# VectorE writes K's transposed blocks with the two heads apart, and the scores read 64-byte runs

## The chip, the cores and the metric

The kernel runs on one core of one Trainium2 chip. The metric is the device time of one execution in microseconds (us). The core's engines are named as the profile names them: PE (TensorE, matmuls), PEld (its weight loads), DVE (VectorE), ACT (ScalarE), POOL (GpSimd) and SP (SyncE, which issues nearly all transfers). SBUF is the on-chip memory of 128 partitions, psum the accumulators that matmuls write, and HBM the memory off the chip.

## What is computed

Two attention blocks with cached K and V are computed from inputs of their own, and their outputs are joined along the last axis. Block A has 32 query heads that share 4 heads of K and V; block B has 32 heads of each. In both there are 16 batches of 32 tokens, 1024 model columns, 1024 cached positions and heads of 128 columns, all in bf16.

```python
def _B_ref(x, k_cache, v_cache, wq, wo):      # x 16x32x1024, k_cache and v_cache 16x32x1024x128
    q = (x @ wq).reshape(B, Sq, H, Dh).transpose(0, 2, 1, 3)
    scores = einsum("bhqd,bhkd->bhqk", q, k_cache) * Dh ** -0.5
    p = softmax(scores, axis=-1)
    o = einsum("bhqk,bhkd->bhqd", p, v_cache)
    return o.transpose(0, 2, 1, 3).reshape(B, Sq, H * Dh) @ wo
# _A_ref: the same with 4 heads of k_cache and v_cache, each repeated 8 times
return concatenate([A, B], axis=-1)
```

## The kernel before

Each of the two blocks is cut into 128 steps. A step of A (a quad) takes four query heads of one batch, a step of B two heads of two neighbouring batches; in both these are 128 rows of scores. Two steps of B with the other two of four heads and the same batches form a pair, so B has 64 pairs. The loop in `build` goes through B's pairs and A's quads side by side, and adds the projections of the queries (L735, L754), the output projections (L823) and the loads of weights between them. What is added this way is only a list of operations with their dependences. `list_schedule` then orders the whole list once, before the program is written: it prices each operation by the table `DUR`, each transfer by `PACKET`, and gives every engine a fixed order. `emit_all` writes the engines' programs in that order, with semaphore waits where one engine needs another's result. The change alters no name, dependence or price, so the order stays as it is.

K of B is needed with the head's 128 columns on partitions. A pair needs K of four heads in two batches, which comes in two loads of 1 MB, one for each batch (`st_dmaKB`, L912), each into two neighbouring slots of KB_sb; late in the kernel some go into wq_sb. One load brings four heads `(i e)` of a batch:

```python
src = pb["k"][...].rearrange("(i e) (r s) d -> (e r) i (s d)", e=2, s=32)
```

A partition is made up of e, r and i, with i the innermost: within each 32 partitions there are sixteen r, and for each both heads i = 0 and 1 side by side. Along a partition lie 32 positions s of 128 columns d. `st_ktrB` (L982) then lets VectorE transpose each slot in place as 4-byte words, in blocks of 32x32 (L983). A word is two neighbouring columns d, w = 0 and 1. After it a partition stands for a pair of columns, and the 32 words of a block stand for 16 positions r of head i = 0 and 1 in turn.

`st_scoresB` (L1018) multiplies the queries with it. For each of four passes `fp` (which half of the blocks, and which of the two columns in a word) it issues 16 matmuls on 32x32 tiles of TensorE, each with 512 streamed columns (32 positions s times 16 positions r): four row groups, one for each e and half of the 32 r, times four x, which are the two batches (x // 2) and i = x % 2. Each x takes the words of its own i alone, so its 2-byte elements stand 8 bytes apart. The four passes add up in the same psum banks (L1035).

The scores then go to `st_max` (the maximum on VectorE, L1046), `st_exp` (exp and its sum on ScalarE, L1059), `st_ptB` (TensorE transposes of the probabilities, L1105), copies out of psum on either engine (L651) and the product with V (`st_pvB`, L1124). A's quads take the same way by L976, L1002, L1046, L1059, L1071 and L1091. The queries of B are turned by a smaller transpose on VectorE (L765) and by matmuls with an identity (L778). x is turned at the start by L671, and B's outputs by L1198. SyncE issues the loads in its own order and waits for slots to come free: L912 for K of B, L962 for V of B, L891 and L898 for K and V of A.

Of the kernel before, what the change touches and what calls it, by code (L numbers as in the profile page):

```python
# [11 lines left out]
F32 = mybir.dt.float32  # L12
# [540 lines left out]
def build(nc, pa, pb, out):  # L553
# [32 lines left out]
    pr = Prog()  # L586
    stack = contextlib.ExitStack()
    with stack:
# [35 lines left out]
        def bank(v):  # L624
            return psum[:, v.idx, :]
# [308 lines left out]
        def home_k(x):  # L934
            if x < XK:
                return ("KB", x % NKB)
            return ("wq", (x - XK) % (NKB + 4)) if (x - XK) % (NKB + 4) < 4 else ("KB", kb_of(x))

        def tile_k2(x):
            kind, sl = home_k(x)  # L940
            assert x % 2 == 0 and sl % 2 == 0 and home_k(x + 1) == (kind, sl + 1)
            return (wq_sb[:, 2 * sl:2 * sl + 4, :] if kind == "wq" else KB_sb[:, sl:sl + 2, :]).rearrange("p j c -> p (j c)")

        def tile_k(x):
            kind, sl = home_k(x)
            return wq_sb[:, 2 * sl:2 * sl + 2, :].rearrange("p j c -> p (j c)") if kind == "wq" else KB_sb[:, sl, :]
# [33 lines left out]
                 wtag={("KTA", sl): q.kid})  # L980

        def st_ktrB(x):  # L982
            pr.add("dve", lambda e: e.transpose(tile_k(x).bitcast(F32), tile_k(x).bitcast(F32)),  # L983
                   writes=[home_k(x)], name="KBt_tr", rtag={home_k(x): x}, wtag={home_k(x): ("T", x)})

        def both(vS):
# [2 lines left out]
        def score_buf(q):  # L989
            q.vS = [Virt("bank", "S"), Virt("bank", "S")]  # L990
            q.vst, q.vbo = Virt("stat"), Virt("bank")
# [24 lines left out]
        def st_scoresB(qs):  # L1016
            n = qs[0].pn
            vP, vPT = (("xT", 0, 0), (("xT", 0, 1), ("xT", 0, 2))) if n >= XT_FREE and n % 2 else (Virt("P2"), (Virt("PT2"), Virt("PT2")))  # L1018
            for q in qs:
                score_buf(q)  # L1020
                q.vP, q.vPT, q.vO = vP, vPT, Virt("O2")
            q0 = qs[0]
            gp = (q0.m * NG + q0.G) % 2

            def e_s(e, fp):
                last = None
                o0 = (fp // 2) * 64 + fp % 2
                for x in range(4):
                    for q in qs:
                        for g2 in range(2):  # L1030
                            r0 = 32 * (2 * q.e + g2)
                            lhsT = QR[r0:r0 + 32, gp, 2 * q.bp + x // 2, x % 2, o0:o0 + 63:2]
                            k2 = tile_k2(4 * q.pn + x // 2 * 2)[r0:r0 + 32, :].rearrange("p (s x) -> p s x", s=32)
                            rhs = k2[:, :, o0 + 2 * (x % 2):(fp // 2) * 64 + 64:4]
                            last = e.matmul(bank(q.vS[g2])[32 * x:32 * x + 32, :].rearrange("p (s j) -> p s j", s=32), lhsT, rhs,  # L1035
                                            start=(fp == 0), stop=(fp == 3), tile_position=(r0, 32 * x))
                return last
            qr = [("QR", gp, 2 * q0.bp + t_) for t_ in range(2)]
            kt = [(home_k(4 * q0.pn + x), ("T", 4 * q0.pn + x)) for x in range(4)]
            for fp_ in range(4):  # L1040
                pr.add("pe", lambda e, fp_=fp_: e_s(e, fp_), reads=qr + [r_ for r_, _ in kt], writes=[r_ for q in qs for r_ in q.vS],
                       name="scoresB", tag="B%d" % q0.t, rtag=dict([(r_, (q0.m, q0.G)) for r_ in qr] + kt))
# [174 lines left out]
        def pairB(n):  # L1217
            qs = [quadsB[2 * n], quadsB[2 * n + 1]]
            for x in range(4):
                st_ktrB(4 * n + x)  # L1220
            if n == 0:
                for x in range(4, NKB):
                    st_dmaKB(x)
            st_scoresB(qs)
            while k_next[0] < min(2 * NIT, 4 * n + 4 + NKB + (4 if n >= LATE else 0)):
                st_dmaKB(k_next[0])
                k_next[0] += 1
            if 4 * n == V_LAST - 8:
                for x in (0, 2, 1, 3):
                    st_dmaVB(V_LAST + x)  # L1230
            for q in qs:
                st_max(q)
                st_exp(q)
            st_ptB(qs)
            if 4 * n == V_LAST:
                st_last(qs)
                return
            st_pvB(qs)
            while v_next[0] < min(V_LAST, 4 * n + 4 + NVB + (4 if n >= LATE else 0)):
                st_dmaVB(v_next[0])  # L1240
                v_next[0] += 1
            for q in qs:
                st_recip(q)
                st_norm(q)
                st_otr(q)
# [122 lines left out]
        if SCHED:  # L1368
            pr = pr.list_schedule()
# [41 lines left out]
```

## Time and profile before

| | before |
|---|---|
| median of 3 runs | 895.69 us (893.65 to 896.92) |
| the profiled execution's own time | 897.08 us |
| its span | 895.3 us |
| mean granted TensorE clock | 0.996 |
| PE, DVE, ACT busy | 819.3, 741.0, 617.9 us |
| moved by DMA | 341.66 MB, mean 382 GB/s |

The span runs from the first to the last instruction; the profiled execution's own time is 1.8 us more. Busy times of engines overlap. In the groups of instructions, a row names line, engine, operation, output<-inputs and shapes, then the count, the busy time in all, the mean duration of one in ns, and the idle time of the engine just before them with what ended it. A busy time counts overlapping matmuls once, so it is less than count times duration. A few matmul records can be missing.

### The profile page before, as it was taken

The page shows a single profiled execution, that of the slowest core. Times are in us where ns is not written, and L with a number is a line of the kernel's source. Part 1 is how long each engine was busy: PE and PEld are TensorE (multiplying, and loading weights), DVE is VectorE, ACT ScalarE, POOL GpSimd, SP SyncE. Part 2 cuts the span into 40 slices and gives each one's busy share as a digit, 9 for nine tenths or more (in the row PEclk, how much of TensorE's full clock was granted, in tenths as well). Part 3 has the DMA queues.
Part 4 walks back from the last instruction along what each step waited for, and adds up shares of the span by engine and source line. Part 5 has one row for each costly group of instructions (what it writes and reads, how often), then busy time and mean ns, then how long its engine had stood idle before and what let it go on. Part 6 is the DMA issues. An engine that isn't in the chain of part 4 may idle for free.

```text
span 895.3 us, 29488 instructions
## 1 busy us (share of the span) xinstructions
PE 819.3 (92%) x12925; PEld 530.3 (59%) x13056; DVE 741.0 (83%) x1039; ACT 617.9 (69%) x1342; POOL 6.1 (1%) x20
## 2 busy tenths in 40 slices
PE   7988999999999999899999999999999998989786
PEld 4445565666665666556666665656656655666554
DVE  0588888788888798887998887998898888899875
ACT  4477687777766775676766777576767667787744
POOL 0000000000000000000000000000000000000000
PEclk9999999999999999999999999999999999999999
DMA  9999999999999999899999999899999999999990
GB/s 338 414 381 392 418 400 383 403 362 386 393 416 387 372 395 382 352 364 410 363 412 371 413 372 391 344 417 394 363 419 404 379 398 413 395 418 417 421 378 37
DMA packets 93775, 341.66 MB, mean 382 GB/s; under 512 B 10000, under 2 KB 10256, under 8 KB 77264
## 3 DMA queue, kind: packets, MB, share of 16 engines
q1 hardware_dynamic: 93088, 337.94, 95.5%
q8 instruction: 103, 1.69, 0.7%
q0 software_dynamic: 560, 1.84, 0.5%
q14 instruction: 24, 0.20, 0.1%
HBM read 337.64 MB, written 2.10 MB: 379 GB/s over the span
## 4 chain that ended last, share of the span: by engine, by line
PE 64%; ACT 15%; DVE 14%; DMA 4%; issue 2%; SPq 1%; DVEq 0%; ACTq 0%
PE psum L1035 14%; PE psum L823 10%; ACT P_sb L1059 9%; DVE stat L1046 9%; PE psum L1124 9%; PE psum L1105 5%; PE psum L1071 5%; PE psum L735 5%; PE psum L1091 4%; PE psum L754 4%; PE psum L1002 4%; DVE KB_sb L983 3%; DMA VB_sb<-in_B_v_cache_dram 2%; PE psum L976 2%; ACT O_sb L1182 1%
## 5 line engine op out<-in xcount | busy, mean ns | idle before, releaser
L1046 DVE TENSOR_REDUCE stat<-psum 128x1 f32<-128x1024 f32 x256 | 305.2, 1215 | 80.1 <-PE psum L1035 51.9
L1059 ACT ACTIVATE P_sb<-psum,stat 128x1024 bf16<-128x1024 f32 x246 | 275.5, 1120 | 104.5 <-DVE stat L1046 101.3
L983 DVE STREAM_TRANSPOSE KB_sb<-KB_sb 128x1024 f32<-128x1024 f32 x240 | 285.6, 1220 | 14.3 <-DMA KB_sb<-in_B_k_cache_dram 14.2
L651 ACT COPY PT_sb<-psum 128x512 f32<-128x512 f32 x217 | 125.4, 601 | 40.2 <-PE psum L1071 21.2
L1035 PE MATMUL psum<-KB_sb,QR 32*32 32x512 bf16 x3840 | 125.9, 630 | 5.9 <-ACT P_sb L1059 3.3
L1124 PE MATMUL psum<-VB_sb,PT_sb 64*64 64x256 bf16 x3584 | 116.6, 271 | 7.5 <-ACT P_sb L1059 3.1
L1124 PEld LDWEIGHTS psum<-VB_sb,PT_sb 64*64 64x64 bf16 x3584 | 96.5, 107 | 29.1 <-issue 26.5
L1182 ACT ACTIVATE O_sb<-psum,stat 128x128 bf16<-128x128 f32 (+1 forms) x197 | 78.8, 418 | 42.7 <-PE psum L1091 27.6
L1071 PE MATMUL psum<-id,P_sb 128*128 128x128 f32 x512 | 89.1, 298 | 7.1 <-ACT P_sb L1059 3.6
L1071 PEld LDWEIGHTS psum<-id,P_sb 128*128 128x128 f32 x512 | 73.6, 208 | 26.6 <-ACT P_sb L1059 13.2
L1091 PE MATMUL psum<-VA_sb,PT_sb 128*128 128x128 bf16 x1024 | 77.9, 219 | 5.4 <-ACT P_sb L1059 2.0
L1105 PE MATMUL psum<-id,P_sb 128*128 128x128 f32 x472 | 76.8, 288 | 6.1 <-ACT P_sb L1059 5.0
L1091 PEld LDWEIGHTS psum<-VA_sb,PT_sb 128*128 128x128 bf16 x1024 | 62.9, 98 | 30.8 <-issue 11.1
L1035 PEld LDWEIGHTS psum<-KB_sb,QR 32*32 32x32 bf16 x3840 | 50.1, 89 | 52.0 <-issue 21.0
L1002 PE MATMUL psum<-KTA_sb,QT_sb 128*128 128x512 bf16 x202 | 68.8, 380 | 6.8 <-ACT P_sb L1059 2.3
L1105 PEld LDWEIGHTS psum<-id,P_sb 128*128 128x128 f32 x472 | 64.6, 194 | 16.9 <-ACT P_sb L1059 7.6
L754 PE MATMUL psum<-wq_sb,xT_sb 128*128 128x512 bf16 x239 | 68.6, 388 | 4.5 <-DMA wq_sb<-in_B_wq_dram 2.2
L823 PE MATMUL psum<-woB_sb,OTB_sb 128*128 128x512 bf16 x234 | 62.4, 379 | 4.6 <-issue 1.6
L823 PE MATMUL psum<-woA_sb,OTA_sb 128*128 128x512 bf16 x241 | 61.2, 388 | 3.0 <-issue 1.4
L735 PE MATMUL psum<-xT_sb,wq_sb 128*128 128x512 bf16 x170 | 48.2, 379 | 2.5 <-issue 1.8
L1059 ACT ACTIVATION_READ_ACCUMULATOR P_sb<-psum,stat 128x1 f32 x246 | 49.7, 202 | 0.0
L835 DVE TENSOR_TENSOR acc<-acc,psum 128x512 f32<-128x512 f32 x64 | 41.1, 675 | 6.2 <-PE psum L823 5.9
(74 smaller groups left out, 737.0 us busy)
## 6 DMA issues: line engine op xcount, KB each, us to landing
KB_sb<-in_B_k_cache_dram SPq DMA_DIRECT2D x120, 1024.0 KB, 8.6
VB_sb<-in_B_v_cache_dram SPq DMA_DIRECT2D x234, 512.0 KB, 8.1
KA_sb<-in_A_k_cache_dram SPq DMA_DIRECT2D x64, 256.0 KB, 7.3
VA_sb<-in_A_v_cache_dram SPq DMA_DIRECT2D x64, 256.0 KB, 7.4
wq_sb<-in_B_wq_dram SPq DMA_DIRECT2D x16, 512.0 KB, 8.0
woB_sb<-in_B_wo_dram SPq DMA_DIRECT2D x32, 256.0 KB, 8.9
woA_sb<-in_A_wo_dram SPq DMA_DIRECT2D x32, 256.0 KB, 7.7
wq_sb<-in_B_k_cache_dram SPq DMA_DIRECT2D x8, 1024.0 KB, 12.0
```

The lines of the kernel that those rows point to most:

```text
L651: return e.copy(dst, src) if hasattr(e, "activation") else e.tensor_copy(dst, src)
L754: last = e.matmul(bank(v)[:, 0:CW], xT_sb[:, 1, j, G * P:(G + 1) * P], wq_sb[:, j, mh * CW:(mh + 1) * CW], start=(j == 0), stop=(j == DJ - 1))
L823: last = e.matmul(bank(v)[:, 0:OUTW], OT[:, gp, hh, :], wo_[:, hh, oh * OUTW:(oh + 1) * OUTW], start=(hh == 0), stop=(hh == nh - 1))
L983: pr.add("dve", lambda e: e.transpose(tile_k(x).bitcast(F32), tile_k(x).bitcast(F32)), writes=[home_k(x)], name="KBt_tr", rtag={home_k(x): ...
L1002: pr.add("pe", lambda e, u=u: e.matmul(bank(vS[u]), qt[:, q.b, q.hh0:q.hh0 + 4, :].rearrange("p a q -> p (a q)"), KTA_sb[:, sl, u * 512:(u ...
L1035: last = e.matmul(bank(q.vS[g2])[32 * x:32 * x + 32, :].rearrange("p (s j) -> p s j", s=32), lhsT, rhs, start=(fp == 0), stop=(fp == 3), t ...
L1046: pr.add("dve", lambda e: e.tensor_reduce(stat[:, vst.idx, 0:1], both(vS), AXIS.XY, ALU.max, negate=True), writes=vS + [vst], name="max")
L1059: return e.activation(dst, src, ACTF.Exp, bias=stat[:, vst.idx, 0:1], scale=1.0, accum_out=stat[:, vst.idx, 1:2])
L1071: last = e.transpose(bank(vb)[:, m * P:(m + 1) * P], p32[:, m:Sk // 2:NPK], id32[:])
L1091: last = e.matmul(bank(vb)[:, 0:Dh], ptc_of(vPT, c, 0, P), VA_sb[:, kvs, c, :], start=(c == 0), stop=(c == NCH - 1))
L1105: last = e.transpose(bank(vb)[:, m * P:(m + 1) * P], p32[:, 4 * h + m:Sk:8], id32[:])
L1124: last = e.matmul(bank(q.vbo)[n0:n0 + 64, 0:2 * Dh].rearrange("p (i d) -> p i d", i=2), pt2_chunk(vPT, c, e0, n0), v2[e0:e0 + 64, :, c, :] ...
```

## The change

VectorE's transpose of a slot of K reads as before but writes through another pattern: within each block of 32 words, word 2b + i goes to place 16i + b. So a block holds the 16 positions of head i = 0 in its first 64 bytes and those of head i = 1 in the other 64. The scores of x read the half with i = x % 2: for each s and each half f, 16 elements of 2 bytes that stand 4 bytes apart, within 64 bytes. Number and sizes of instructions, transfers and buffers stay the same.

```diff
         def st_ktrB(x):
-            pr.add("dve", lambda e: e.transpose(tile_k(x).bitcast(F32), tile_k(x).bitcast(F32)),
+            def emit(e):
+                t32 = tile_k(x).bitcast(F32)
+                return e.transpose(t32.rearrange("p (k i b) -> p k b i", i=2, b=16), t32.rearrange("p (k b i) -> p k b i", i=2, b=16))
+            pr.add("dve", emit,
                    writes=[home_k(x)], name="KBt_tr", rtag={home_k(x): x}, wtag={home_k(x): ("T", x)})
...
                             lhsT = QR[r0:r0 + 32, gp, 2 * q.bp + x // 2, x % 2, o0:o0 + 63:2]
-                            k2 = tile_k2(4 * q.pn + x // 2 * 2)[r0:r0 + 32, :].rearrange("p (s x) -> p s x", s=32)
-                            rhs = k2[:, :, o0 + 2 * (x % 2):(fp // 2) * 64 + 64:4]
+                            k2 = tile_k2(4 * q.pn + x // 2 * 2)[r0:r0 + 32, :].rearrange("p (s f i b w) -> p s f i b w", s=32, f=2, i=2, b=16)
+                            rhs = k2[:, :, fp // 2, x % 2, :, fp % 2]
```

## The prediction

> **What bounds the kernel now.** I read the page first, then the busy time in three stretches, then the waits of VectorE and of SyncE's queue.
>
> ```profile
> span 895.3 us, 29488 instructions
> ## 1 busy us (share of the span) xinstructions
> PE 819.3 (92%) x12925; PEld 530.3 (59%) x13056; DVE 741.0 (83%) x1039; ACT 617.9 (69%) x1342; POOL 6.1 (1%) x20
> ...
> GB/s 338 414 381 392 418 400 383 403 362 386 393 416 387 372 395 382 352 364 410 363 412 371 413 372 391 344 417 394 363 419 404 379 398 413 395 418 417 421 378 37
> ...
> q1 hardware_dynamic: 93088, 337.94, 95.5%
> ...
> ## 4 chain that ended last, share of the span: by engine, by line
> PE 64%; ACT 15%; DVE 14%; DMA 4%; issue 2%; SPq 1%; DVEq 0%; ACTq 0%
> PE psum L1035 14%; PE psum L823 10%; ACT P_sb L1059 9%; DVE stat L1046 9%; PE psum L1124 9%; PE psum L1105 5%; PE psum L1071 5%; PE psum L735 5%; PE psum L1091 4%; PE psum L754 4%; PE psum L1002 4%; DVE KB_sb L983 3%; DMA VB_sb<-in_B_v_cache_dram 2%; PE psum L976 2%; ACT O_sb L1182 1%
> ```
>
> Three things stand near their limit together: TensorE is busy for 92% of the span, VectorE for 83%, and the main DMA queue for 95.5% of the sixteen engines' time. The chain that ended last runs mostly over TensorE, and its largest single line is the scores of B, L1035, with 14% of 895.3 us, or 125 us. DMA is 4% of that chain.
>
> ```profile
> 0.00:40.00 40.00, 32.79 (x217) 16.69 (x236) 10.20 (x11) 16.28 (x24) 2.15 (x13) 1.00 0.97 374
> 40.00:840.00 800.00, 744.15 (x11928) 487.16 (x12017) 692.58 (x973) 574.25 (x1260) 2.31 (x4) 1.00 0.99 391
> 840.00:895.30 55.30, 42.38 (x800) 26.45 (x804) 38.22 (x57) 27.38 (x60) 1.63 (x3) 0.94 0.61 248
> ```
>
> The columns are the length, the busy time of PE, PEld, DVE, ACT and POOL, the granted clock, the DMA share and GB/s. The middle stretch of 800 us is the steady state. VectorE works 692.6 us of it and stands idle for 107.4 us. That idle time is all that VectorE can take up before it sets the pace itself. TensorE is idle there for 55.9 us, and the DMA share is 0.99. The clock is full, so every duration below can be compared with every other.
>
> ```profile
> DVE stat L1046 <- PE psum L1035: 51.9, 50, 3.0
> DVE stat L1046 <- PE psum L1002: 17.3, 30, 2.4
> DVE KB_sb L983 <- DMA KB_sb<-in_B_k_cache_dram: 14.2, 11, 5.3
> ```
>
> Half of VectorE's spare time is spent waiting for the scores of B: 51.9 us in 50 waits, or 1.04 us each. VectorE hardly ever waits for K itself (14.2 us).
>
> ```profile
> SPq L962 <- PE psum L1124: 128.3, 43, 9.8
> SPq L891 <- PE psum L976: 76.5, 29, 6.6
> ```
>
> SyncE's queue waits for TensorE to release buffers (128.3 us for V of B alone, 76.5 us for K of A). So TensorE decides when most loads start, although the DMA engines are almost never empty.
>
> **The scores: what the change gives.** The rows of one line, grouped by shape, and one run of it in the timeline:
>
> ```profile
> L1035 PE MATMUL psum<-KB_sb,QR 32*32 32x512 bf16 x3840 | 125.9, 630 | 5.9 <-ACT P_sb L1059 3.3 <-ACT OTB_sb L651 0.7 <-ACT OTA_sb L651 0.5
> L1002 PE MATMUL psum<-KTA_sb,QT_sb 128*128 128x512 bf16 x202 | 68.8, 380 | 6.8 <-ACT P_sb L1059 2.3 <-issue 1.0 <-ACT PT_sb L651 0.9
> L778 PE MATMUL psum<-QBt,ident 32*32 32x256 bf16 x512 | 20.0, 279 | 3.0 <-ACT PT_sb L651 0.7
> L1198 PE MATMUL psum<-rowsel,O_sb 128*128 128x128 bf16 x252 | 27.3, 220 | 1.2 <-ACT O_sb L1182 0.8
> ```
>
> ```profile
> 398.14 2.11 PE L1035 MATMUL psum<-KB_sb,QR 32*32 32x512 bf16 x64 [0.48 <-ACT P_sb L1059]
> ```
>
> ```profile
> 40.00:840.00 800.00, 125.59 (x3840) 49.95 (x3808) 1.00 0.99 391
> 840.00:895.30 55.30, 8.28 (x256) 3.36 (x256) 0.94 0.61 248
> ```
>
> One score step of a pair is 64 matmuls on 32x32 tiles, four (the four passes `fp`) behind one another on each of 16 tiles. One takes 630 ns with 512 columns. On contiguous operands 512 columns take 380 ns (L1002) and 128 columns 220 ns (L1198), so a column costs 160/384 = 0.417 ns, and 256 columns should take 273 ns. L778 uses the same 32x32 tiles with contiguous moving columns and takes 279 ns for 256. So the small tile costs nothing, and the 250 ns that L1035 takes above 380 ns come from how it reads K: one 2-byte element every 8 bytes. The run of 64 in 2.11 us says the same: (2.11 - 0.63)/3 = 0.49 us from pass to pass, where 512 columns at 0.417 ns are 0.213 us.
>
> After the change the step is 4 bytes, sixteen elements in 64 bytes. No matmul row in the trace moves its streamed operand at this step. The weights of L1035 itself are read at a 4-byte step, which gives no price for a stream. The bounds are therefore no gain (630 ns stay) and the full 250 ns; I take the full one, since the data per element is as dense as can be without repacking the two halves of a word, and half the step should at least halve a cost that comes with the step. A run then loses 4 x 0.25 = 1.0 us, and all 64 runs lose 64 us of TensorE's 819. The middle stretch holds 3840/64 = 60 recorded runs, 60 us. None of this appears in the time unless VectorE keeps up.
>
> The Trainium skill, "SBUF — State Buffer", section "Door 1: The DMA port swizzle", says that two hits on one 16-byte line are enough for full bandwidth. An 8-byte step has two hits per line, so by that rule the scores would be at full rate already and this part would give nothing; the 630 ns against 380 ns speak against it.
>
> **The transposes: what the change costs.** Every one of the 256 transposes of K (240 in KB_sb, 16 in wq_sb) keeps its source order and its count. Its destination changes: two successive elements of a block, which lay 4 bytes apart, now go to places 64 bytes apart, then 60 bytes back, and so on through all 1024.
>
> ```profile
> L983 DVE STREAM_TRANSPOSE KB_sb<-KB_sb 128x1024 f32<-128x1024 f32 x240 | 285.6, 1220 | 14.3 <-DMA KB_sb<-in_B_k_cache_dram 14.2
> L765 DVE STREAM_TRANSPOSE QBt<-Qtok 128x256 f32<-128x256 f32 x32 | 13.6, 426 | 15.1 <-ACT Qtok L649 13.3 <-PE psum L778 1.8
> ```
>
> ```profile
> 0.00:40.00 40.00, 4.74 (x4) 1.00 0.97 374
> 40.00:840.00 800.00, 282.49 (x238) 1.00 0.99 391
> 840.00:895.30 55.30, 16.89 (x15) 0.94 0.61 248
> ```
>
> From 256 to 1024 elements the time grows from 426 to 1220 ns, or 1.034 ns per element, with 162 ns fixed. The streamed part is 1059 ns. No VectorE row in this trace writes with such hops, so I price it from both sides. The cheap side is another engine's stream that hops 64 bytes and more, in PSUM:
>
> ```profile
> L1059 ACT ACTIVATE P_sb<-psum,stat 128x1024 bf16<-128x1024 f32 x246 | 275.5, 1120 | 104.5 <-DVE stat L1046 101.3
> L651 ACT COPY PT_sb<-psum 128x512 f32<-128x512 f32 x217 | 125.4, 601 | 40.2 <-PE psum L1071 21.2 <-PE psum L1105 17.0
> L651 ACT CAST OTB_sb<-psum 128x128 bf16<-128x128 f32 x110 | 25.9, 280 | 7.3 <-PE psum L1198 6.7
> ```
>
> ScalarE's exp reads its 1024 scores across the grain. Its copies and casts, which read in longer runs, grow by (601 - 280)/384 = 0.84 ns per element; on to 1024 elements that gives 1029 ns, and exp takes 1120 ns. A hop costs at most 0.09 ns per element there. Carried to VectorE this is 0.09 us per transpose, and the lower bound is nothing at all. I exclude a gain: the count is the same and the destination only less orderly. The dear side is TensorE reading SBUF:
>
> ```profile
> L671 PEld LDWEIGHTS psum<-ident,acc 128*128 128x128 bf16 x64 | 5.2, 152 | 4.3 <-DMA acc<-in_B_x_dram 3.7 <-issue 0.3
> L976 PEld LDWEIGHTS psum<-ident,KA_sb 128*128 128x128 bf16 x512 | 31.6, 98 | 9.6 <-issue 5.5 <-DMA KA_sb<-in_A_k_cache_dram 1.3
> ```
>
> L671 loads 128 columns at a 16-byte step in 152 ns, where L976 loads contiguous ones in 98 ns. That is 0.42 ns more per element, or 1.55 times. L1035 above pays (0.49 - 0.213)/512 = 0.54 ns per element, or 2.3 times. Carried over as nanoseconds, these are 0.43 and 0.55 us per transpose; as factors on 1059 ns they are 0.58 and 1.38 us. I take 0.58 us, the factor of L671: it is the row in which, as in the new write, every element lies in another 16 bytes than the one before, in the same memory. A transpose then takes 1.80 us. The ends are 0 and 1.38 us.
>
> The Trainium skill, "Vector Engine (DVE) Microarchitecture Reference", section "5.2 Measured stream behaviour on trn2", holds that a VectorE port keeps its rate only in runs of two or more adjacent words. Its figures for a hopping destination are 1.71 to 2.50 ns per element against 1.054, so by estimate 0.66 to 1.45 us more per transpose, and in the sum below 993 to 1190 us. It reports too that one source alternating between two regions ran at full rate, and no row here shows a hopping write of VectorE.
>
> **The sum, against the profiled execution.** In the middle stretch VectorE then works 692.6 + 238 x 0.58 = 831 us, more than the 800 us that the stretch has, so it becomes the bound. Its order is fixed, so the maxima (L1046), the reciprocals and the accumulations of both halves stand queued behind the longer transposes; behind the maxima wait ScalarE's exps, then TensorE, and SyncE's loads behind TensorE. No wait is added and no instruction or transfer is moved. Of its idle 107.4 us the 51.9 us of waiting for scores go, because runs are 1 us shorter and a late VectorE finds them done. Of the other 55 us I keep 40: some are waits for TensorE and DMA that shrink when VectorE is late, some are round trips that stay. The middle takes 831 + 40 = 871 us, 71 more. Outside it, four transposes stand ahead of the first scores, and about eight on the path at the end: 12 x 0.58 = 7 us, less two score runs, 2 us; 5 us more. The span is 895.3 + 71 + 5 = 971 us. The profiled execution's own time is 897.08 us, 1.8 above its span and 1.4 above the median of 895.69, so I forecast 973 in its terms and 972 us as a median. With 0.43 us per transpose and 28 us of idle the middle is 823, the end 3, and the time 922. With 1.38 us it is 692.6 + 328 + 40 = 1061 and 15 at the ends, the time 1172.
>
> **Rivals.** *The write is free* and the kernel is faster. This decides if the hop costs below about 0.15 us per transpose, so that 238 of them fit in the half of VectorE's idle time that the scores do not give back. For it speaks exp's cheap hop, and that both lines of a pair of halves are revisited on alternate elements. Against it speak both TensorE rows. VectorE could then finish the middle in 692.6 + 55 = 748 us and TensorE in 744 - 60 + 56 = 740. Loads would be next late: at a share of 0.99 they leave room only for 1%, 792 us; at the 421 GB/s of the page's best slice (row above), against 391, the same bytes take 743. So the middle lies between 748 and 792, and the ends give 2 to 4: with the 1.8 us, 841 to 887 us; I take 868, nearer the DMA's side, since its share has so little left.
>
> *The scores gain nothing*, because a 4-byte step in short runs is as slow as an 8-byte one, and the write is free too. Then the time stays at 896 us. The contiguous 279 ns of L778 speaks against it only in part, being step 2 bytes. The same case covers gain and cost that cancel: with about 0.3 us per transpose VectorE needs 692.6 + 71 + 40 = 804 in the middle.
>
> *The hop costs more than any row here*, above 1.38 us. Then VectorE's middle alone exceeds 1021 us and the time passes 1172. Nothing in this trace asks for it.
>
> **How the numbers follow.** I give 0.63 to the forecast with its ends 922 to 1172, 0.27 to the free write, 0.04 to no change and 0.06 to the dearer hop. A difference of 0.5%, some 4.5 us, is about what a measurement can tell from none. So slower is 0.69, the same 0.04 and faster 0.27. The range may leave out two tenths: the dearer hop (0.06) and the faster half of the free write (0.13). It is 868 to 1172. The likeliest case alone has 922 to 1172.
>
> **What would show it.** L983 should take about 1.8 us, with the same count; below 1.3 us the forecast is wrong and the free write right. L1035 should fall from 630 to about 385 ns, a run of 64 from 2.11 to about 1.1 us. VectorE's busy time should be near 890 us and over nine tenths in nearly every slice, its waits for L1035 almost gone, the chain mostly VectorE, and the mean DMA rate near 350 GB/s. If L983 is slow and the time is nevertheless under 900, then VectorE's idle time was cheaper to fill than I hold.

## The result, and the profile after

| | before | after |
|---|---|---|
| median | 895.78 us (893.65 to 896.92, 4 runs) | 975.75 us (974.78 to 978.5, 4 runs) |
| ratio to before | | 1.0901 (95% interval 1.087 to 1.0931) |
| the profiled execution's span | 895.3 us | 974.5 us |
| its own time | 897.08 us | 976.24 us |

The change makes the kernel 9% slower. The forecast was 972 us, with a range of 868 to 1172. The lines of the changed file from the transposes on stand lower by two or three: L985 is the transpose of K (L983 before), L1038 the scores of B (L1035), L1049 the maximum (L1046), L1062 the exp (L1059) and L1127 the product with V (L1124).

The page of the changed kernel, the same parts as were shown of before, with the granted clock by slice:

```profile
span 974.5 us, 29488 instructions
## 1 busy us (share of the span) xinstructions
PE 803.7 (82%) x12925; PEld 539.0 (55%) x13056; DVE 889.9 (91%) x1039; ACT 619.7 (64%) x1342; POOL 6.1 (1%) x20
...
PEclk9978999999998999999989998899999999989898
...
q1 hardware_dynamic: 93088, 337.94, 89.5%
...
## 4 chain that ended last, share of the span: by engine, by line
DVE 66%; PE 25%; ACT 5%; issue 2%; DMA 2%; SPq 0%; DVEq 0%; ACTq 0%
DVE KB_sb L985 36%; DVE stat L1049 20%; ACT P_sb L1062 4%; PE psum L1038 4%; PE psum L1127 4%; PE psum L823 3%; DVE wq_sb L985 3%; PE psum L754 2%; PE psum L1074 2%; DVE acc L835 2%; PE psum L735 2%; PE psum L1094 2%; PE psum L1108 2%; PE psum L1005 2%; DVE O_sb L1186 1%
```

VectorE has gone from 83% to 91% of a longer span, and the chain has moved to it: 66% where it was 14%, with the transposes alone at 36%. TensorE is busy for 15.6 us less: its scores take 49.4 us less (134.2 to 84.8 us, with those in wq_sb), its other work some 34 us more, at a lower granted clock (0.954 on the mean, 0.996 before). The main DMA queue has room now, 89.5%.

The costliest groups, by shape, and the waits of VectorE that answer to those shown of before:

```profile
L985 DVE STREAM_TRANSPOSE KB_sb<-KB_sb 128x1024 f32<-128x1024 f32 x240 | 446.5, 1923 | 4.7 <-DMA KB_sb<-in_B_k_cache_dram 4.6
L1038 PE MATMUL psum<-KB_sb,QR 32*32 32x512 bf16 x3840 | 79.2, 422 | 19.2 <-ACT P_sb L1062 4.6 <-DVE KB_sb L985 3.8 <-DVE acc L835 3.4
L1062 ACT ACTIVATE P_sb<-psum,stat 128x1024 bf16<-128x1024 f32 x246 | 274.6, 1117 | 176.1 <-DVE stat L1049 173.1
```

```profile
DVE stat L1049 <- PE psum L1038: 16.5, 20, 2.8
DVE KB_sb L985 <- DMA KB_sb<-in_B_k_cache_dram: 4.6, 1, 4.6
```

Both halves of the change did what was expected of them. A transpose takes 1923 ns instead of 1220. A score matmul takes 422 ns on the mean instead of 630. But VectorE's work grew by more than TensorE's shrank. VectorE now waits 16.5 us for the scores instead of 51.9, and ScalarE's exp waits 173.1 us for VectorE's maxima, where the row of before has 101.3.

The durations of transposes overlap a little, so their true cost is read from start to start. The timeline has three in a row in each kernel, first before, then after:

```profile
459.02 3.49 DVE L983 STREAM_TRANSPOSE KB_sb<-KB_sb 128x1024 f32<-128x1024 f32 x3
```

```profile
439.08 5.39 DVE L985 STREAM_TRANSPOSE KB_sb<-KB_sb 128x1024 f32<-128x1024 f32 x3
```

Before, the two later ones add (3.49 - 1.22)/2 = 1.14 us each; after, (5.39 - 1.92)/2 = 1.73 us. The difference is 0.60 us. VectorE's busy time as a whole rose by 889.9 - 741.0 = 148.9 us, which is 0.58 us for each of 256.

### The profile page after: what moved, and what is told of

Same layout as the page of the kernel before. It is cut to its first block, busy times and chain, and to the rows that moved or that the text cites. A ratio compares the mean times of both kernels' runs of the same rounds, so it can differ in the third digit from the quotient of the medians.

```text
span 974.5 us, 29488 instructions
## 1 busy us (share of the span) xinstructions
PE 803.7 (82%) x12925; PEld 539.0 (55%) x13056; DVE 889.9 (91%) x1039; ACT 619.7 (64%) x1342; POOL 6.1 (1%) x20
## 3 DMA queue, kind: packets, MB, share of 16 engines
q1 hardware_dynamic: 93088, 337.94, 89.5%
## 4 chain that ended last, share of the span: by engine, by line
DVE 66%; PE 25%; ACT 5%; issue 2%; DMA 2%; SPq 0%; DVEq 0%; ACTq 0%
DVE KB_sb L985 36%; DVE stat L1049 20%; ACT P_sb L1062 4%; PE psum L1038 4%; PE psum L1127 4%; PE psum L823 3%; DVE wq_sb L985 3%; PE psum L754 2%; PE psum L1074 2%; DVE acc L835 2%; PE psum L735 2%; PE psum L1094 2%; PE psum L1108 2%; PE psum L1005 2%; DVE O_sb L1186 1%
## 5 line engine op out<-in xcount | busy, mean ns | idle before, releaser
L985 DVE STREAM_TRANSPOSE KB_sb<-KB_sb 128x1024 f32<-128x1024 f32 x240 | 446.5, 1923 | 4.7 <-DMA KB_sb<-in_B_k_cache_dram 4.6
L1062 ACT ACTIVATE P_sb<-psum,stat 128x1024 bf16<-128x1024 f32 x246 | 274.6, 1117 | 176.1 <-DVE stat L1049 173.1
L1049 DVE TENSOR_REDUCE stat<-psum 128x1 f32<-128x1024 f32 x256 | 302.0, 1205 | 27.4 <-PE psum L1038 16.5
L1127 PE MATMUL psum<-VB_sb,PT_sb 64*64 64x256 bf16 x3584 | 125.2, 283 | 18.3 <-ACT P_sb L1062 11.6
L1127 PEld LDWEIGHTS psum<-VB_sb,PT_sb 64*64 64x64 bf16 x3584 | 103.2, 112 | 39.6 <-issue 35.5
L1074 PE MATMUL psum<-id,P_sb 128*128 128x128 f32 x512 | 93.5, 308 | 27.1 <-ACT P_sb L1062 16.1
L1074 PEld LDWEIGHTS psum<-id,P_sb 128*128 128x128 f32 x512 | 75.2, 209 | 48.9 <-ACT P_sb L1062 28.1
L1038 PE MATMUL psum<-KB_sb,QR 32*32 32x512 bf16 x3840 | 79.2, 422 | 19.2 <-ACT P_sb L1062 4.6
L1108 PE MATMUL psum<-id,P_sb 128*128 128x128 f32 x472 | 79.1, 294 | 11.0 <-ACT P_sb L1062 5.3
L754 PE MATMUL psum<-wq_sb,xT_sb 128*128 128x512 bf16 x239 | 72.4, 406 | 8.1 <-DMA wq_sb<-in_B_wq_dram 3.2
L1108 PEld LDWEIGHTS psum<-id,P_sb 128*128 128x128 f32 x472 | 66.2, 195 | 21.5 <-ACT P_sb L1062 7.2
L1038 PEld LDWEIGHTS psum<-KB_sb,QR 32*32 32x32 bf16 x3840 | 44.9, 90 | 50.4 <-issue 7.4
L1062 ACT ACTIVATION_READ_ACCUMULATOR P_sb<-psum,stat 128x1 f32 x246 | 48.8, 198 | 0.0
L976 PE MATMUL psum<-ident,KA_sb 128*128 128x128 bf16 x512 | 40.2, 223 | 3.9 <-ACT PT_sb L651 2.0
```

What stands on the lines that cost most here:

```text
L754: last = e.matmul(bank(v)[:, 0:CW], xT_sb[:, 1, j, G * P:(G + 1) * P], wq_sb[:, j, mh * CW:(mh + 1) * CW], start=(j == 0), stop=(j == DJ - 1))
L985: return e.transpose(t32.rearrange("p (k i b) -> p k b i", i=2, b=16), t32.rearrange("p (k b i) -> p k b i", i=2, b=16))
L1049: pr.add("dve", lambda e: e.tensor_reduce(stat[:, vst.idx, 0:1], both(vS), AXIS.XY, ALU.max, negate=True), writes=vS + [vst], name="max")
L1062: return e.activation(dst, src, ACTF.Exp, bias=stat[:, vst.idx, 0:1], scale=1.0, accum_out=stat[:, vst.idx, 1:2])
L1074: last = e.transpose(bank(vb)[:, m * P:(m + 1) * P], p32[:, m:Sk // 2:NPK], id32[:])
L1108: last = e.transpose(bank(vb)[:, m * P:(m + 1) * P], p32[:, 4 * h + m:Sk:8], id32[:])
```

## The experiments

Two theories stood at first: that VectorE pays for the hopping destination itself, or that TensorE's denser reads of SBUF disturb VectorE's transposes. The first two kernels do one half of the change each. The third keeps the aim of the change but gives VectorE runs of two words, the fourth makes the hop short. The last four ask which side of a transpose pays and for which distance, how the idle time of VectorE is filled, and how much of the loss is a matter of order.

### The reads alone

```diff
-                return e.transpose(t32.rearrange("p (k i b) -> p k b i", i=2, b=16), t32.rearrange("p (k b i) -> p k b i", i=2, b=16))
+                return e.transpose(t32, t32)
```

> The scores read as after the change, the transposes write as before it, so the scores multiply columns of the wrong head. Theory 1 (the hopping write is what costs): the transposes fall back to 1.22 us, the scores stay at about 390 ns, and the time is that of the prediction's rival, 841 to 887 us. Theory 2 (TensorE's denser reads disturb VectorE's transposes in SBUF): the transposes stay near 1.9 us and the time near 975 us. If DMA leaves no room: 1.22 us, 390 ns and about 890 us.

Measured: 855.26 us, 0.9577 of before (0.9538 to 0.9616).

```profile
L985 DVE STREAM_TRANSPOSE KB_sb<-KB_sb 128x1024 f32<-128x1024 f32 x240 | 285.9, 1221 | 20.3 <-DMA KB_sb<-in_B_k_cache_dram 19.9
L1038 PE MATMUL psum<-KB_sb,QR 32*32 32x512 bf16 x3840 | 72.9, 389 | 6.5 <-ACT P_sb L1062 3.2 <-ACT OTA_sb L651 1.1 <-ACT OTB_sb L651 0.8
```

```profile
q1 hardware_dynamic: 93088, 337.94, 98.4%
```

The transposes are back at 1.22 us beside scores at 389 ns. So TensorE's denser reads do not slow VectorE, and theory 2 falls. The gain of the reads is real: some 41 us, once VectorE can follow. The DMA queue stands at 98.4%, so there is little more to have behind it.

### The write alone

```diff
-                            k2 = tile_k2(...)[r0:r0 + 32, :].rearrange("p (s f i b w) -> p s f i b w", s=32, f=2, i=2, b=16)
-                            rhs = k2[:, :, fp // 2, x % 2, :, fp % 2]
+                            k2 = tile_k2(...)[r0:r0 + 32, :].rearrange("p (s x) -> p s x", s=32)
+                            rhs = k2[:, :, o0 + 2 * (x % 2):(fp // 2) * 64 + 64:4]
```

> The transposes write as after the change, the scores read as before it, again columns of the wrong head. Theory 1: transposes 1.9 us, scores 630 ns, and since VectorE is the bound the 64 us that TensorE loses again hardly show: 975 to 1000 us. Theory 2: transposes 1.22 us and the time of before, 896 us.

Measured: 994.2 us, 1.111 of before (1.108 to 1.1139).

```profile
L985 DVE STREAM_TRANSPOSE KB_sb<-KB_sb 128x1024 f32<-128x1024 f32 x240 | 449.8, 1937 | 6.0 <-DMA KB_sb<-in_B_k_cache_dram 6.0
L1038 PE MATMUL psum<-KB_sb,QR 32*32 32x512 bf16 x3840 | 125.2, 629 | 21.8 <-DVE KB_sb L985 6.1 <-ACT P_sb L1062 4.6 <-DVE acc L835 3.8
```

The write alone lengthens the transposes, to 1.94 us, with the scores as slow as ever. It costs 98 us, and the reads then win back 18 of them (994.2 to 975.75). On their own the same reads win 41. The two halves do not add up to the whole: where VectorE sets the pace, over half of TensorE's gain is not seen.

### Runs of two words

```diff
-                return e.transpose(t32.rearrange("p (k i b) -> p k b i", i=2, b=16), t32.rearrange("p (k b i) -> p k b i", i=2, b=16))
+                return e.transpose(t32.rearrange("p (k i r t) -> p k r i t", i=2, r=8, t=2), t32.rearrange("p (k r i t) -> p k r i t", i=2, r=8, t=2))
...
-                src = pb["k"][...].rearrange("(i e) (r s) d -> (e r) i (s d)", e=2, s=32)
-                pr.add("sp", lambda e: e.dma_start(tile_k2(x), src), ...
+                src = pb["k"][...].rearrange("(i e) (r t s) d -> t (e r) i (s d)", e=2, t=2, s=32)
+                pr.add("sp", lambda e: [e.dma_start(tile_k2(x)[t::2, :], src[t]) for t in range(2)], ...
```

Both transfers of a load raise the same semaphore, and its waits count both.

> K comes in two transfers per load, so that two neighbouring positions r of a head lie on neighbouring partitions; the transpose then writes runs of two words (8 bytes) in turn to the two halves of a block, and the scores read as after the change. The whole result is computed. Theory 1, with the Trainium skill's rule that runs of two adjacent words keep the rate ("Vector Engine (DVE) Microarchitecture Reference", section 5.2): transposes 1.22 us, scores 390 ns, 841 to 887 us. Theory 1 with a cost for each hop: half as many hops, 0.3 us more per transpose, about 1.55 us, and a time of 890 to 915 us. The 128 transfers that are added cost SyncE's queue 0.3 to 0.5 us each and nothing on the path.

Measured: 859.35 us, 0.9619 of before (0.9582 to 0.9656), so faster than both kernels.

```profile
L986 DVE STREAM_TRANSPOSE KB_sb<-KB_sb 128x1024 f32<-128x1024 f32 x240 | 286.1, 1222 | 21.4 <-DMA KB_sb<-in_B_k_cache_dram 21.4
L1039 PE MATMUL psum<-KB_sb,QR 32*32 32x512 bf16 x3840 | 73.2, 390 | 6.4 <-ACT P_sb L1063 3.2 <-issue 1.0 <-ACT OTB_sb L652 0.7
```

```profile
PE 769.2 (90%) x12925; PEld 525.3 (61%) x13056; DVE 737.9 (86%) x1039; ACT 616.9 (72%) x1342; POOL 6.1 (1%) x20
...
q1 hardware_dynamic: 95136, 337.95, 98.5%
...
PE 51%; DVE 20%; ACT 14%; DMA 12%; issue 3%; SPq 1%; DVEq 0%; ACTq 0%
```

With two neighbouring words per hop the transpose costs 1222 ns, as without any hop (1220), although the halves are still 64 bytes apart. So a hop after each pair is free; a single word between two hops is what costs. The forecast of a cost per hop (1.55 us) is refuted. The scores keep their 390 ns. The 128 added transfers do not show: 859 against the 855 of the reads alone, with intervals that overlap. The queue is at 98.5%, and the chain runs mostly over TensorE again (51%).

### A hop within 16 bytes

```diff
-                return e.transpose(t32.rearrange("p (k i b) -> p k b i", i=2, b=16), t32.rearrange("p (k b i) -> p k b i", i=2, b=16))
+                return e.transpose(t32.rearrange("p (k a i b) -> p k a b i", a=8, i=2, b=2), t32.rearrange("p (k a b i) -> p k a b i", a=8, i=2, b=2))
...
+                            k2 = tile_k2(...)[r0:r0 + 32, :].rearrange("p (s f a i b w) -> p s f a i b w", s=32, f=2, a=8, i=2, b=2)
+                            rhs = k2[:, :, fp // 2, :, x % 2, :, fp % 2]
```

> The transpose sorts the two heads only within every 4 words: each word goes 8 bytes on or 4 bytes back, always inside 16 bytes, and the scores read pairs of elements 4 bytes apart, every 16 bytes. The whole result is computed. If what costs is that every word lies in another 16 bytes than the one before, as the prediction took it: transposes 1.22 us and, if the scores reach 390 ns, 841 to 887 us. If the neighbouring word must come next: about 1.9 us and about 975 us. Scores: 390 ns if two words of 8 bytes are read in turn at full rate, 630 ns if the 16-byte step counts.

Measured: 896.01 us, 1.0 of before (0.998 to 1.0019).

```profile
L985 DVE STREAM_TRANSPOSE KB_sb<-KB_sb 128x1024 f32<-128x1024 f32 x240 | 285.7, 1221 | 13.9 <-DMA KB_sb<-in_B_k_cache_dram 13.6
L1038 PE MATMUL psum<-KB_sb,QR 32*32 32x512 bf16 x3840 | 125.7, 630 | 6.3 <-ACT P_sb L1062 3.3 <-DVE acc L835 1.0 <-ACT OTB_sb L651 0.7
```

Words are written in the order 0, 2, 1, 3, then 4, 6, 5, 7, and the transpose costs 1221 ns. The two words of one 8-byte pair never follow one another, so such pairs are not needed. That the write stays in the same 16 bytes for four words is one reading that fits. Another is not excluded: 2 and 1 are neighbours too, and so are 3 and 4, so a rule that two neighbours must come in turn, in either direction and from any word, fits this kernel and the others as well.

The scores show the other side: they read two elements 4 bytes apart out of every 16 bytes and take the same 630 ns as before, when the two stood 8 bytes apart. So it is not the step between neighbouring elements that counts for TensorE's stream. What goes with the time is how many elements it takes from each 16 bytes: two cost 630 ns, four cost 389 with the reads alone, and all eight 380 in L1002 (there on one 128x128 tile). In both slow layouts the two heads, which are separate streams, also take their elements from the same 16 bytes, in the fast ones from different ones. No run separates the two.

### Half of the slots

```diff
             def emit(e):
                 t32 = tile_k(x).bitcast(F32)
+                if x % 4 >= 2:
+                    return e.transpose(t32, t32)
...
                             rhs = k2[:, :, fp // 2, x % 2, :, fp % 2]
+                            if x // 2 == 1:
+                                k2 = tile_k2(...)[r0:r0 + 32, :].rearrange("p (s x) -> p s x", s=32)
+                                rhs = k2[:, :, o0 + 2 * (x % 2):(fp // 2) * 64 + 64:4]
```

> Only the slots of the first of the two batches are written with the heads apart, and the scores read each batch as its slots were written; the whole result is computed. It asks how the idle time of VectorE is filled. The prediction's accounting: 128 longer transposes cost 74 us of VectorE, the middle stretch has 692.6 + 119 x 0.58 = 762 us of work, 40 us of idle time stay, and the stretch is about 800 us as before: 896 to 905 us. Rival (VectorE's lateness is passed on wherever a chain runs over it, whether or not it has idle time elsewhere): half of the loss of the whole change, about 935 us. In both, transposes of 1.22 and 1.92 us; the scores of a run wait for their slower half, so 64 matmuls gain little.

Measured: 931.1 us, 1.0375 of before (1.0354 to 1.0395).

```profile
L987 DVE STREAM_TRANSPOSE KB_sb<-KB_sb 128x1024 f32<-128x1024 f32 x120 | 228.1, 1941 | 12.0 <-DMA KB_sb<-in_B_k_cache_dram 12.0
L986 DVE STREAM_TRANSPOSE KB_sb<-KB_sb 128x1024 f32<-128x1024 f32 x120 | 142.9, 1217 | 0.0
L1043 PE MATMUL psum<-KB_sb,QR 32*32 32x512 bf16 x3840 | 124.3, 504 | 12.3 <-ACT P_sb L1067 3.4 <-DVE acc L835 2.1 <-DVE KB_sb L986 1.9
```

```profile
40.00:870.00 830.00, 760.37 (x12010) 490.56 (x11985) 759.35 (x970) 571.59 (x1251) 2.30 (x4) 0.99 0.96 378
```

Half of the longer transposes cost 33.5 us. The stretch has 759 us of VectorE's work, as forecast (762), but lasts 830 and not 800: 71 us of idle time stay, not 40. So the accounting fails: VectorE's idle time does not take up longer transposes until it is used up.

The rival named the time, 935 us, but by a comparison that is not like for like. It halved the loss of the whole change, 80 us, in which the gain of the reads is contained. Here a run of scores waits for its slower half, TensorE is busy with the scores for 124.3 us (125.9 before), and that gain is missing. The kernel to compare with is the write alone:

```profile
PE 839.9 (90%) x13056; PEld 536.5 (58%) x13056; DVE 816.7 (88%) x1039; ACT 618.0 (66%) x1342; POOL 6.1 (1%) x20
PE 839.8 (85%) x12925; PEld 536.4 (54%) x13056; DVE 894.8 (90%) x1039; ACT 618.9 (62%) x1342; POOL 6.1 (1%) x20
```

The first row is this kernel, the second the write alone; before, VectorE was busy for 741.0 us. The first half of the longer transposes adds 76 us of VectorE's work and 34 us to the span (895.3 to 929.7 us), the second half another 78 us of work and 62.5 us of span (to 992.2). VectorE's idle time over the whole span falls from 154 us to 113 and then to 97. So idle time takes up over half of the first addition and a fifth of the second. Both expectations are too simple: neither is all of it used first, nor is lateness passed on in equal parts. A likely reason, which no run shows by itself, is that a pair whose transposes are late has its scores, maxima and exps late, and the idle time of another pair is of little use to it.

### A hop of 16 bytes

```diff
-                return e.transpose(t32.rearrange("p (k i b) -> p k b i", i=2, b=16), t32.rearrange("p (k b i) -> p k b i", i=2, b=16))
+                return e.transpose(t32.rearrange("p (k a i b) -> p k a b i", a=4, i=2, b=4), t32.rearrange("p (k a b i) -> p k a b i", a=4, i=2, b=4))
```

The scores read this layout in the manner of the kernel with the hop within 16 bytes, with a=4 and b=4.

> The heads are sorted within every 8 words: each word goes 16 bytes on or 12 bytes back, so always to another 16 bytes than the word before, and the scores read four elements 4 bytes apart and skip 16 bytes. The whole result is computed. If the 16 bytes decide, for writes and for reads: transposes 1.92 us, scores 390 ns, 976 us as with the change. If the distance of the hop matters (64 bytes are far, 16 near): transposes between 1.22 and 1.92 us, 855 to 975 us.

Measured: 994.13 us, 1.1077 of before (1.1027 to 1.1127).

```profile
L985 DVE STREAM_TRANSPOSE KB_sb<-KB_sb 128x1024 f32<-128x1024 f32 x240 | 470.6, 2026 | 6.0 <-DMA KB_sb<-in_B_k_cache_dram 6.0
L1038 PE MATMUL psum<-KB_sb,QR 32*32 32x512 bf16 x3840 | 78.1, 418 | 24.6 <-ACT P_sb L1062 5.7 <-DVE KB_sb L985 5.7 <-DVE acc L835 4.5
```

When nearly every word lies in other 16 bytes than the one before and beside neither the word before nor the one after it, the write is slow: 2026 ns, even 0.10 us more than with hops of 64 bytes, and the time is worse than with the change. Why the near hop costs a little more than the far one is open. The scores, with four elements from each 16 bytes that they touch, run at 418 ns on the mean (median 392), at a mean granted clock of 0.958.

### The hop on the source

```diff
-                return e.transpose(t32.rearrange("p (k i b) -> p k b i", i=2, b=16), t32.rearrange("p (k b i) -> p k b i", i=2, b=16))
+                return e.transpose(t32.rearrange("p (k b i) -> p k b i", i=2, b=16), t32.rearrange("p (k i b) -> p k b i", i=2, b=16))
```

The scores read as before the change.

> The transpose reads its words with the hop of 64 bytes and writes them in order; the scores read as before the change, so the column pairs of K are permuted against those of the queries. It asks whether VectorE pays for a hopping source as for a hopping destination. If it does: transposes 1.92 us and about 994 us, as when only the write was changed. If only writes pay: 1.22 us and 896 us.

Measured: 897.99 us, 1.001 of before (0.9987 to 1.0034).

```profile
L985 DVE STREAM_TRANSPOSE KB_sb<-KB_sb 128x1024 f32<-128x1024 f32 x240 | 292.6, 1249 | 13.6 <-DMA KB_sb<-in_B_k_cache_dram 13.6
```

The same hop in the words that VectorE reads adds 29 ns to 1220, and the time is that of before. The dear side is the write.

### The true price in the planner

```diff
-    "KBt_tr": (1.15, 0.11), ...
+    "KBt_tr": (1.70, 0.11), ...
```

> The kernel with the change, but its planner prices a transpose of K at 1.70 us instead of 1.15, so it orders the work for the longer transposes; the whole result is computed. If the loss is the work that VectorE has too much of: its busy time stays near 890 us and the time within 960 to 980 us. If a good part of it is an order planned for shorter transposes: VectorE's idle time of 85 us shrinks and the time falls to 930 us or less.

Measured: 954.55 us, 1.0642 of before (1.0613 to 1.0671).

```profile
PE 815.1 (86%) x13056; PEld 529.2 (56%) x13056; DVE 859.4 (90%) x978; ACT 641.4 (67%) x1403; POOL 6.1 (1%) x20
```

Both expectations miss, and the answer lies between them: 21 of the 80 us come back. VectorE's idle time does not shrink at all (952.3 - 859.4 = 93 us); its work does, by 30 us, because the planner gives 61 operations more to ScalarE (978 instructions on VectorE instead of 1039, 1403 on ScalarE instead of 1342). So about a quarter of the loss can be won back by a plan that knows the price, and it is won by moving work from VectorE to ScalarE, not by less idle time. Whether the same plan would also help the kernel before was not tried, so this quarter is not shown to be the fault of a plan made for shorter transposes.

## Why the prediction was right, point by point

**The price of the transpose.** Forecast: 0.58 us more, 1.80 in all. Measured: 0.58 us in VectorE's busy time, 0.60 from start to start, 1.923 as a duration that overlaps its neighbours. The figure is right, but the way to it was not sound, and that it came out so close is luck. It was carried over from TensorE's weight loads, which read SBUF. VectorE reading the same hop pays 0.03 us (the hop on the source), and its writes pay only in the two layouts in which single words go to other 16 bytes (64 bytes on, or 16). What held of the reasoning is that choice of row: "every element lies in another 16 bytes". That the ratio of 1.55 carried over from a read on one engine to a write on another is not explained by any run here.

**The sum in the middle stretch.** The busy times in three stretches of the changed kernel, in the columns of those shown of before:

```profile
0.00:40.00 40.00, 32.33 (x193) 16.35 (x196) 11.21 (x10) 14.89 (x21) 2.14 (x13) 1.00 0.97 373
40.00:915.00 875.00, 730.21 (x11940) 495.74 (x12060) 831.11 (x974) 577.64 (x1264) 2.30 (x4) 0.96 0.93 360
915.00:974.50 59.50, 41.17 (x796) 26.95 (x802) 47.61 (x58) 27.20 (x60) 1.62 (x3) 0.88 0.52 197
```

Forecast were 831 us of work and 40 us of idle time. The stretch from 40 to 915 us has 831.1 us of work and 43.9 us of idle time. The step that failed lies behind that sum: "That idle time is all that VectorE can take up before it sets the pace itself". With half of the longer transposes 71 us of idle time were left in the stretch, and the kernel was 34 us slower all the same. The sum came out because with all of them VectorE sets the pace for most of the time (66% of the chain) and the idle time that stays happens to be near the 40 us that were kept. Those 40 us were a choice among 55, which no row gave; that they hit is luck in part. The price given for no change, about 0.3 us per transpose with the gain of the scores, was not tried: half of the slots has a mean of 0.29 us, but without that gain, and loses 3.75%. The point given for the free write, 0.15 us, was not tried either.

**The scores.** Forecast: 385 ns, 1.1 us per run of 64, and 64 us of TensorE's busy time. With the reads alone the scores take 56 us less (134.2 to 78.2 us). Of the changed kernel's runs, two:

```profile
416.05 1.22 PE L1038 MATMUL psum<-KB_sb,QR 32*32 32x512 bf16 x64
```

```profile
507.73 1.94 PE L1038 MATMUL psum<-KB_sb,QR 32*32 32x512 bf16 x64
```

The first is at full clock: (1.22 - 0.39)/3 = 0.28 us from pass to pass, where it was 0.49. The second ran at a granted clock of 0.50; the page's row of the clock has slices at 7 and 8 tenths, and the mean is 0.954 against 0.996. That was not foreseen and accounts for the mean of 422 ns: sorted by the clock granted while they ran, the 3456 score matmuls at full clock take 389 ns, the 592 at half clock 618. With the reads alone, at a mean clock of 0.994, the mean is 389. The lower clock is hardly what made the kernel slow: TensorE is only 25% of the chain in the changed kernel, and with the write alone the clock was higher, 0.976, and the time longer.

**SBUF's rule for the scores.** The Trainium skill's rule of two hits per 16 bytes ("SBUF — State Buffer", section "Door 1: The DMA port swizzle") was set aside for TensorE's stream, and rightly: two elements per 16 bytes cost 630 ns in two layouts. For VectorE's writes the runs agree with it: two words per 16 bytes before the next hop are at full rate (1222 ns), one is not (1923 and 2026 ns). The Trainium skill's rule of two or more adjacent words that start on an 8-byte boundary ("Vector Engine (DVE) Microarchitecture Reference", section "5.2 Measured stream behaviour on trn2") is stricter than what was measured: in the order 0, 2, 1, 3 the two words of an 8-byte pair never come in turn, and it costs nothing (1221 ns). The estimate that the prediction worked out from the figures of that section, 0.66 to 1.45 us more per transpose (over 1024 words they give 0.67 to 1.48), lies above the 0.60 us measured.

**The rivals.** The free write was priced at 841 to 887 us, with 868 taken. With the reads alone, where the write is free, it was 855, and with runs of two words 859. The DMA left a little more room than was assumed: the queue is at 98.4 and 98.5% in these two. VectorE's waits for the scores fell to 16.5 us, less far than the "almost gone" of the prediction.

## What to carry to other kernels

Before a layout is mended for the engine that reads it, price the write that makes it in the trace of the engine that must do it. On VectorE look at what lies between two hops of the destination: two 4-byte words side by side were free, one was not, and a different order of the load gave both engines what they wanted. An engine's idle time over a whole stretch is the most that longer work can use. Here the first 76 us of added work used 41 us of it, and the kernel was 34 us slower with 113 us of idle time still there.

## What the runs showed of the hardware that was not expected

VectorE's stream transpose reads words in hops of 64 bytes almost freely (1249 ns against 1220) but pays 0.6 us per 1024 words when it writes them so. TensorE's streamed operand went with the number of 2-byte elements used in each 16 bytes: on 32x32 tiles, with four streams on each row group, two gave 630 ns for 512 columns and four 389; all eight, on one 128x128 tile, gave 380. The slow layout did not get slower at half clock: with the write alone, 172 score matmuls at a granted clock of 0.50 took 630 ns, those at full clock 629, while the denser layout went from 389 to 618. So at full clock the slow layout is held up by something other than the granted clock of TensorE.

And the granted clock was lower where TensorE was busy for less of the span: 0.989 or more on the mean in the runs with 90% or more, 0.970 and 0.976 at 86 and 85%, 0.958 and 0.954 at 83 and 82%. Why it goes with the busy share is not shown.
